# Landmark attention and two MLPs on one Trainium2 core: stores on another queue, less elementwise work on GpSimd, one chain for the inverse

## Chip, cores and metric

The kernel runs on one core of a Trainium2 chip. The metric is device time in microseconds (us). TensorE (PE) multiplies matrices, VectorE (DVE) and ScalarE (ACT) work elementwise, GpSimd (POOL) does some elementwise steps and issues transfers, SyncE (SP) only issues transfers.

## What is computed

Three stages follow one another; the output of one is the input of the next.

```python
# attention, B, H, S, D = 4, 8, 576, 64; 32 landmarks, each the mean of 18 rows
A  = softmax(scale * q    @ k_lm.T)      # 576 x 32 per head
Bm = softmax(scale * q_lm @ k_lm.T)      # 32 x 32
C  = softmax(scale * q_lm @ k.T)         # 32 x 576
Z  = Bm.T / (norm1(Bm) * norminf(Bm) + 1e-6)
for _ in range(6):
    Z = 2 * Z - Z @ Bm @ Z               # approximate inverse of Bm
x = A @ Z @ C @ v                        # heads side by side: 2304 x 512
# first MLP, 512 -> 1536 -> 512
x = (sigmoid(x @ w_gate) * (x @ w_val)) @ w_out
# second MLP, 512 -> 2048 -> 512
h = x @ w_in
out = (max(h, 0) + alpha * min(h, 0)) @ w_out2
```

The weights arrive as 8-byte floats; the rest is 4-byte.

## The kernel before

**Attention.** It runs per batch b, in two groups j of four heads. `transposed` brings k and q into a transposed layout and forms the landmark means. `landmark_scores` and `landmark_exp` give Bm; `att_values` gives C @ v (tile Cv); `att_queries` gives A, split into two float32r parts. `newton(b, j)` computes the inverse of one group: after a preamble of small VectorE steps, six steps, each with four 32-row matmuls on the diagonal (L396), a ScalarE copy (L426) and a VectorE add (L427, the last one L432). Z and Cv are multiplied to M (L442). A and M are never multiplied with the weights of the first MLP apart: `fold` forms We = M @ w (matmul L578), so that layer 1 is A @ We.

For batch 0 the six parts (inverse, queries, values, each for two groups) are interleaved by `together`, one yield of each in turn. The attention of later batches is spread over the blocks of the first MLP, a pace setting how many yields go into one block; the inverse of these has a higher priority in the scheduler (`urgent`). Each engine takes its instructions in a fixed order that the scheduler worked out at build time from program order, priorities and its own estimates.

**Weights.** Each 8-byte weight tile is loaded by SP (`raw`) and narrowed to 4 bytes by `narrow`: one or two ScalarE steps (L128, L132), and on VectorE L137 and L140, with L134 in place of L132 for some. `split` makes two float32r parts: a ScalarE cast (L113) and a subtraction (L114) that goes to VectorE or, with `lo="pool"`, to GpSimd. The gate and value weights are also stored in DRAM (`wgvd`, L556) and reloaded for later batches by GpSimd's queue (L564). The folded weights of batch 3 are stored (`we3d`) and taken back by `take_stored`. `narrow_w2` prepares the second MLP's weights during the first: load, narrow into tile n, store to `w2d` (L670).

**First MLP.** There are 24 blocks per batch (12 column chunks f for each of two halves of 288 rows). A block is `layer1` (12 matmuls, L616), the sigmoid (L627), a product (L628) and a split, then `layer2` (12 matmuls, L635) two blocks later. Finished tiles xs are stored to `x2d` (L726). **Second MLP**: `load_x2` reads x2d and splits it (the subtraction on GpSimd), `layer3` (L812) and `layer4` (L830) follow.

Before the change every store is issued on SP's queue, in which the loads also stand, and an issue that waits holds what is behind it. The code that the change touches:

Of the kernel before, what the change touches and what calls it, by code (L numbers as in the profile page):

```python
# [21 lines left out]
def tile_landmark_attention_glu_prelu(  # L22
# [240 lines left out]
    def value_scores(b, j, ps_tile):  # L263
# [4 lines left out]
        for half in range(2):  # L268
# [10 lines left out]
    def value_exp(b, j):  # L279
# [6 lines left out]
        for half in range(2):  # L286
            nc.scalar.activation(
                e[:, half * HB : (half + 1) * HB], pc[half][:, :HB], AF.Exp,
                bias=mx[:, 2:3], scale=SCALE, accum_out=den[:, half : half + 1],
            )  # L290
# [45 lines left out]
    def query_scores(b, j, ps_tile):  # L336
# [21 lines left out]
    def query_rest(b, j):
# [28 lines left out]
    def newton(b, j, ps_tile):  # L387

        bm = att[b, j, "B"]
        bt = apool.tile([P, LM], F32, tag="bt", name="bt", bufs=2)  # L390
        nc.vector.transpose(out=bt, in_=bm)

        def diag(ps, lhsT, rhs, n):
            for h in range(4):
                s = slice(32 * h, 32 * h + 32)
                nc.tensor.matmul(ps[s, :n], lhsT=lhsT[s], rhs=rhs[s], start=True, stop=True)  # L396

        pb = ps_tile("psbb")
        diag(pb, bm, bm, LM)
        sums = apool.tile([P, 2], F32, tag="sums", name="sums", bufs=2)  # L400
        nc.vector.tensor_reduce(out=sums[:, 0:1], in_=bm, axis=AX.X, op=ALU.add)
        nc.vector.tensor_reduce(out=sums[:, 1:2], in_=bt, axis=AX.X, op=ALU.add)
        st = apool.tile([P, 2, LM], F32, tag="st", name="st", bufs=2)
        sp = apool.tile([P, 2, LM], F32, tag="sp", name="sp", bufs=2)
        nc.vector.tensor_copy(sp, sums[:, :, None].to_broadcast([P, 2, LM]))
        nc.vector.transpose(
            out=st.rearrange("p a l -> p (a l)"), in_=sp.rearrange("p a l -> p (a l)")
        )
        nm = apool.tile([P, 2], F32, tag="nm", name="nm", bufs=2)
        nc.vector.tensor_reduce(out=nm, in_=st, axis=AX.X, op=ALU.max)  # L410
        nr = apool.tile([P, 1], F32, tag="nr", name="nr", bufs=2)
        nc.vector.tensor_scalar(
            out=nr, in0=nm[:, 0:1], scalar1=nm[:, 1:2], scalar2=1e-6, op0=ALU.mult, op1=ALU.add
        )
# [1 line left out]
        rz = apool.tile([P, 2, LM], F32, tag="rz", name="rz", bufs=4)
        nc.vector.tensor_scalar(out=rz[:, 1], in0=bt, scalar1=nr, scalar2=None, op0=ALU.mult)
        nc.vector.tensor_scalar(out=rz[:, 0], in0=pb[:, :LM], scalar1=nr, scalar2=None, op0=ALU.mult)
        nc.vector.tensor_tensor(out=rz[:, 0], in0=eye, in1=rz[:, 0], op=ALU.subtract)
# [497 lines left out]
```

## Time and profile before

| | |
|---|---|
| median of 3 runs | 903.42 us (900.98 to 907.16) |
| the profiled execution | 905.6 us, span 903.8 us, mean granted TensorE clock 0.969 |
| PE busy | 856.2 us (95%) |
| DVE busy | 519.8 us (58%) |
| ACT busy | 339.3 us (38%) |
| POOL busy | 98.1 us (11%) |
| DMA | 106.92 MB, mean 118 GB/s |

The span runs from the first to the last instruction. The rows further down name a line of the kernel, an engine, an operation and its tiles as output<-input; "[... <-X]" at the end of a row is the time for which the engine had been idle just before, and the instruction that ended the wait.

### The profile page before, as it was taken

How to read it: one execution, taken by the hardware profiler on the slowest of the kernel's cores; microseconds unless marked ns; L12 is line 12 of the kernel's file. 1: busy time of each engine (PE TensorE's matmuls, PEld its weight loads, DVE VectorE, ACT ScalarE, POOL GpSimd, SP SyncE). 2: the span in 40 equal slices, each digit the busy share in tenths (PEclk: the TensorE clock that was granted, in tenths of full speed). 3: DMA queues.
4: the chain of work that ended last, by engine and by line, in shares of the span. 5: the costliest groups of instructions: out<-in, count | busy, mean ns of one | idle time of the engine just before them, and what ended most of it. 6: DMA issues, size and time to landing. Idle time of an engine off the chain costs nothing.

```text
span 903.8 us, 15276 instructions
## 1 busy us (share of the span) xinstructions
PE 856.2 (95%) x5969; PEld 705.6 (78%) x5969; DVE 519.8 (58%) x1113; ACT 339.3 (38%) x729; POOL 98.1 (11%) x98
## 2 busy tenths in 40 slices
PE   5789888989999999999999999999999999999997
PEld 3347666757778877998899888888888888888896
DVE  5789998668767443576745653443344433444443
ACT  4755856357745433555434421121112111111111
POOL 3301313111111010124100020110010001000000
PEclk8589999979999999999999999999999999999999
DMA  9767777787523252687824420030002000100100
GB/s 257 214 212 233 218 251 203 261 250 229 175 56 103 72 166 95 208 292 231 273 78 119 153 71 1 2 91 1 1 24 58 1 1 12 48 0 1 28 20 24
DMA packets 85161, 106.92 MB, mean 118 GB/s; under 512 B 35664, under 2 KB 57184, under 8 KB 85088
## 3 DMA queue, kind: packets, MB, share of 16 engines
q1 hardware_dynamic: 81632, 93.36, 34.5%
q0 software_dynamic: 3456, 12.58, 4.4%
q8 instruction: 47, 0.77, 0.4%
q14 instruction: 26, 0.21, 0.1%
HBM read 78.65 MB, written 27.26 MB: 117 GB/s over the span
## 4 chain that ended last, share of the span: by engine, by line
PE 76%; DMA 11%; DVE 8%; issue 2%; ACT 1%; POOL 1%; SPq 0%; DVEq 0%; POOLq 0%; ACTq 0%
PE h L812 22%; PE o L830 22%; PE gv L616 12%; PE acc L635 11%; DMA raw<-in_moe_w_out_dram 4%; PE psf L578 4%; DMA raw<-in_moe_w_val_dram 2%; DMA w2d<-n 2%; DVE raw L137 1%; DMA raw<-in_moe_w_in_dram 1%; PE psz L396 1%; DMA tv<-in_v_dram 1%; DVE n L140 1%; PE psa L218 1%; PE psq L191 1%
## 5 line engine op out<-in xcount | busy, mean ns | idle before, releaser
L616 PE MATMUL gv<-A,we 128*128 128x288 f32 x1152 | 194.6, 308 | 7.0 <-ACT g L627 5.4
L616 PEld LDWEIGHTS gv<-A,we 128*128 128x128 f32 x1152 | 164.4, 193 | 41.2 <-issue 27.9
L635 PE MATMUL acc<-gs,wconv 128*128 128x288 f32 x1152 | 184.2, 302 | 6.6 <-DVE gs L114 4.8
L812 PE MATMUL h<-x,w 128*128 128x512 f32 (+1 forms) x840 | 183.7, 368 | 0.0
L635 PEld LDWEIGHTS acc<-gs,wconv 128*128 128x128 f32 x1152 | 162.9, 191 | 19.5 <-issue 10.6
L830 PE MATMUL o<-w,g2s 128*128 128x512 f32 x702 | 170.0, 389 | 0.0
L812 PEld LDWEIGHTS h<-x,w 128*128 128x128 f32 x840 | 148.0, 188 | 27.2
L830 PEld LDWEIGHTS o<-w,g2s 128*128 128x128 f32 x702 | 131.0, 188 | 26.6
L113 ACT CAST g2s<-g 128x512 fp32r<-128x512 f32 (+1 forms) x80 | 46.3, 578 | 276.3 <-DVE g L822 276.3
L818 DVE TENSOR_SCALAR g<-h,alphaT 128x512 f32<-128x512 f32 (+1 forms) x80 | 55.8, 697 | 154.0 <-PE h L812 153.9
L114 DVE TENSOR_TENSOR g2s<-g,g2s 128x512 fp32r<-128x512 f32 (+1 forms) x80 | 55.9, 699 | 55.9 <-ACT g2s L113 55.3
L628 DVE TENSOR_TENSOR g<-g,gv 128x288 f32<-128x288 f32 x96 | 43.0, 448 | 34.4 <-PE gv L616 30.6
L128 ACT ACTIVATE raw<-raw 128x512 f32<-128x512 f32 x68 | 46.6, 686 | 41.2 <-DMA raw<-in_moe_w_in_dram 19.2
L114 DVE TENSOR_TENSOR gs<-g,gs 128x288 fp32r<-128x288 f32 x96 | 48.7, 508 | 21.6 <-ACT gs L113 20.8
L114 POOL TENSOR_TENSOR x<-xr,x 128x512 fp32r<-128x512 f32 (+1 forms) x20 | 24.1, 1218 | 315.3 <-ACT x L113 315.3
L627 ACT ACTIVATE g<-gv 128x288 f32<-128x288 f32 x96 | 39.4, 410 | 47.3 <-PE gv L616 44.9
L137 DVE SCALAR_TENSOR_TENSOR raw<-raw 128x512 uint32<-128x512 uint32 x68 | 51.1, 758 | 9.8 <-ACT raw L132 8.8
L113 ACT CAST gs<-g 128x288 fp32r<-128x288 f32 x96 | 41.4, 432 | 40.5 <-DVE g L628 40.4
L822 DVE SCALAR_TENSOR_TENSOR g<-h,g 128x512 f32<-128x512 f32 (+1 forms) x80 | 51.0, 638 | 2.7
L578 PE MATMUL psf<-wgv,m 64*32 64x512 f32 x384 | 46.2, 629 | 2.2 <-DVE ta L343 1.4
L114 DVE TENSOR_TENSOR we<-psf,we 128x512 fp32r<-128x512 f32 x36 | 23.9, 687 | 19.3 <-ACT we L113 19.2
L113 ACT CAST we<-psf 128x512 fp32r<-128x512 f32 x36 | 20.1, 587 | 32.1 <-PE psf L578 32.1
(134 smaller groups left out, 761.1 us busy)
## 6 DMA issues: line engine op xcount, KB each, us to landing
raw<-in_moe_w_out_dram SPq DMA_DIRECT2D x28, 512.0 KB, 5.8
wgv<-wgvd POOLq DMA_DIRECT2D x24, 512.0 KB, 5.8
raw<-in_moe_w_in_dram SPq DMA_DIRECT2D x16, 512.0 KB, 5.1
w2d<-n SPq DMA_DIRECT2D x32, 256.0 KB, 2.8
st<-w2d SPq DMA_DIRECT2D x32, 256.0 KB, 2.7
raw<-in_moe_w_gate_dram SPq DMA_DIRECT2D x24, 256.0 KB, 4.1
raw<-in_moe_w_val_dram SPq DMA_DIRECT2D x24, 256.0 KB, 4.6
wgvd<-wgv SPq DMA_DIRECT2D x12, 512.0 KB, 6.1
```

Source lines behind the costliest of these rows:

```text
L113: nc.scalar.copy(dst[:, 0, :], src)
L114: (nc.gpsimd if lo == "pool" else nc.vector).tensor_tensor(out=dst[:, 1, :], in0=src, in1=f32(dst[:, 0, :]), op=ALU.subtract)
L128: nc.scalar.activation(w[:, :, 1], w[:, :, 1], AF.Copy, scale=2.0 ** -112)
L137: nc.vector.scalar_tensor_tensor(out=lo, in0=hi, scalar=0x80000000, in1=lo, op0=ALU.bitwise_and, op1=ALU.bitwise_or)
L578: nc.tensor.matmul(pss[j][LM * h : LM * h + LM], lhsT=att[b, j, "M"][d, u], rhs=wgv[c, j][d, u], start=True, stop=True,)
L616: nc.tensor.matmul(ps[:, :HB], lhsT=We[b, c, j][:, a, 256 * i + P * s : 256 * i + P * s + P], rhs=att[b, j, "A"][half][:, e, :], start=(n ...
L628: nc.vector.tensor_tensor(out=g, in0=g, in1=pss[1][:, :HB], op=ALU.mult)
L635: nc.tensor.matmul(acc[m][:, :HB], lhsT=wout_sb[f][:, a, P * m : P * m + P], rhs=gs[:, e, :], start=(f == f0 and n == 0), stop=(f == f1 - ...
L812: nc.tensor.matmul(ps[:, :n], lhsT=w[:, a, kk], rhs=xs[:, e, kk, :n], start=(i == 0), stop=(i == 11))
L818: nc.vector.tensor_scalar(out=g[:, :n], in0=ps[:, :n], scalar1=0.0, scalar2=alphaT[:, f : f + 1], op0=ALU.min, op1=ALU.mult,)
L822: nc.vector.scalar_tensor_tensor(out=g[:, :n], in0=ps[:, :n], scalar=0.0, in1=g[:, :n], op0=ALU.max, op1=ALU.add)
L830: nc.tensor.matmul(acc, lhsT=gs[:, a, P * t : P * t + P], rhs=w2_out[f][:, e, :], start=(f == 0 and i == 0), stop=(f == NF2 - 1 and i == 2),)
```

## The change

It has these parts.

1. The stores of wgvd, we3d, w2d and x2d are issued by GpSimd's queue in place of SP's.
2. The first MLP's splits and the attention's subtraction and product (L349, L365) go from GpSimd to VectorE; only the splits of `load_x2` stay on GpSimd.
3. In batch 0 the `tok` copies go from VectorE to ScalarE, and the landmark sums are one VectorE reduction over all 576 columns; before, GpSimd added two halves first.
4. The landmarks stay sums: the division by 18 (L208) moves into the scales of the exponentials.
5. `newton` takes both groups, eight heads, in each step, with instructions of twice the width; in batch 0 it has the higher priority, and values come before queries.
6. Tile n (`n2`) always has two buffers; it had one until the attention's pool is released.

```diff
@@ -178,9 +180,7 @@
 
         if b == 0:
             tv = apool.tile([TP, R, 2, D], F32, tag="qkv", name="tok", bufs=4)
-            nc.vector.tensor_copy(
-                tv, pre.pop((nm[0], pr)).rearrange("p h (r d) -> p r h d", r=R)
-            )
+            nc.scalar.copy(tv, pre.pop((nm[0], pr)).rearrange("p h (r d) -> p r h d", r=R))
         else:
             tv = load_pair_tok(src, b, pr, "t" + nm)
         x = small_or_slot(b, [P, S + LM], "qT", nm, 4)
@@ -194,19 +194,11 @@
                     ident[:TP, :TP],
                 )
             nc.scalar.copy(x[:, half * HB : (half + 1) * HB], ps[:, :HB])
-        sm = apool.tile([P, LM], F32, tag="lsum", name="lsum", bufs=2)
-        xr, nr = x[:, :S], R
-        if b == 0:
-            xr, nr = apool.tile([P, HB], F32, tag="xh", name="xh", bufs=2), RH
-            nc.gpsimd.tensor_tensor(out=xr, in0=x[:, :HB], in1=x[:, HB:S], op=ALU.add)
         nc.vector.tensor_reduce(
-            out=sm,
-            in_=xr.rearrange("p (r l c) -> p l r c", r=nr, c=TP // LM),
+            out=x[:, S:],
+            in_=x[:, :S].rearrange("p (r l c) -> p l r c", r=R, c=TP // LM),
             axis=AX.XY,
             op=ALU.add,
-        )
-        nc.vector.tensor_scalar(
-            out=x[:, S:], in0=sm, scalar1=1.0 / G, scalar2=None, op0=ALU.mult
         )
         return x
...
@@ -346,14 +339,14 @@
         t3 = ta.rearrange("p (n l) -> p n l", l=LM)
         am = apool.tile([P, G], F32, tag="am", name="am", bufs=2)
         nc.vector.tensor_reduce(out=am, in_=t3, axis=AX.X, op=ALU.max)
-        nc.gpsimd.tensor_tensor(
+        nc.vector.tensor_tensor(
             out=t3, in0=t3, in1=am[:, :, None].to_broadcast([P, G, LM]), op=ALU.subtract
         )
         att[b, j, "qs"] = ta
 
     def query_exp(b, j):
         ta = att[b, j, "qs"]
-        nc.scalar.activation(ta, ta, AF.Exp, scale=SCALE)
+        nc.scalar.activation(ta, ta, AF.Exp, scale=SCALE1)
 
     def query_rest(b, j):
         ta = att.pop((b, j, "qs"))
@@ -362,14 +355,14 @@
         nc.vector.tensor_reduce(out=asum, in_=t3, axis=AX.X, op=ALU.add)
         nc.vector.tensor_scalar(out=asum, in0=asum, scalar1=1e-9, scalar2=None, op0=ALU.add)
         nc.vector.reciprocal(out=asum, in_=asum)
-        nc.gpsimd.tensor_tensor(
+        nc.vector.tensor_tensor(
             out=t3, in0=t3, in1=asum[:, :, None].to_broadcast([P, G, LM]), op=ALU.mult
         )
         at = apool.tile([P, S], F32, tag="T", name="at", bufs=3)
         nc.vector.transpose(out=at, in_=ta)
         if b < B - 1:
             a2 = bpool.tile([P, 2, S], F32R, tag="A", name="A", bufs=4)
-            split(a2, at, lo="pool" if b == 0 else "dve")
+            split(a2, at)
             att[b, j, "A"] = [a2[:, :, h * HB : (h + 1) * HB] for h in range(2)]
         else:
             att[b, j, "A"] = []
...
@@ -384,68 +377,97 @@
-    def newton(b, j, ps_tile):
+    def newton(b, ps_tile):
+        bm = att.pop((b, "B"))
...
+        def diag(ps, lhsT, rhs):
+            for j in range(2):
+                for h in range(4):
+                    s = slice(32 * h, 32 * h + 32)
+                    to = ps[s, j]
+                    nc.tensor.matmul(to, lhsT=lhsT[s, j], rhs=rhs(s, j), start=True, stop=True)
...
         for i in range(6):
-            ps = ps_tile("psz")
-            zn = apool.tile([P, 2, LM], F32, tag="rz", name="rz", bufs=4)
             if i < 5:
-                diag(ps, rz[:, 0], rz.rearrange("p a l -> p (a l)"), 2 * LM)
-                nc.scalar.copy(zn[:, 0], ps[:, :LM])
-                nc.vector.tensor_tensor(
-                    out=zn[:, 1], in0=rz[:, 1], in1=ps[:, LM : 2 * LM], op=ALU.add
-                )
+                zn = small("rz", 2, 2, LM)
+                ps = psum("psz", 2, 2, LM)
+                diag(ps, rz[:, :, 0], lambda s, j: rz[s, j])
+                nc.scalar.copy(zn[:, :, 0], ps[:, :, 0])
+                zj, pz = zn[:, :, 1], ps[:, :, 1]
             else:
-                diag(ps, rz[:, 0], rz[:, 1], LM)
-                nc.vector.tensor_tensor(out=zn[:, 1], in0=rz[:, 1], in1=ps[:, :LM], op=ALU.add)
+                zj = small("zs", 2, LM)
+                pz = psum("psz", 2, LM)
+                diag(pz, rz[:, :, 0], lambda s, j: rz[s, j, 1])
+            nc.vector.tensor_tensor(out=zj, in0=rz[:, :, 1], in1=pz, op=ALU.add)
             rz = zn
             yield
-        zt = apool.tile([P, LM], F32, tag="zt", name="zt", bufs=2)
-        nc.vector.transpose(out=zt, in_=rz[:, 1])
-
-        pm = [ps_tile(f"psm{u}") for u in range(2)]
-        cv = att[b, j, "Cv"]
-        for u, hh, h in HEADS[j]:
-            s = slice(h * LM, h * LM + LM)
-            nc.tensor.matmul(
-                pm[u][D * hh : D * hh + D, :LM], lhsT=cv[s], rhs=zt[s], start=True, stop=True
-            )
-        m = apool.tile([P, 2, LM], F32, tag="m", name="m", bufs=4)
-        for u in range(2):
-            nc.vector.tensor_copy(m[:, u], pm[u][:, :LM])
-        att[b, j, "M"] = m
+        zt = turned("zt", zj, 2)
...
@@ -510,7 +531,8 @@
         yield from together(*(att_landmarks(0, j, ps_tile) for j in range(2)))
         raw_ahead(RAW0)
         yield from together(
-            *(part(0, j, ps_tile) for part in (newton, att_queries, att_values) for j in range(2))
+            urgent(newton(0, ps_tile)),
+            *(part(0, j, ps_tile) for part in (att_values, att_queries) for j in range(2)),
         )
 
 
@@ -545,7 +567,7 @@
         raw = raws.pop((kind, c, pr))
         if kind == "o":
             t = wout_sb[c] = ws_tile("wconv")
-            split(t, narrow(raw), lo="dve" if c in LO_DVE else "pool")
+            split(t, narrow(raw))
             return
         j, u = divmod(pr, 2)
         if u == 0:
@@ -553,7 +575,7 @@
         t = wgv[c, j]
         narrow(raw, t[:, u], act=True)
         if u == 1:
-            nc.sync.dma_start(out=wgvd[c, j], in_=t)
+            nc.gpsimd.dma_start(out=wgvd[c, j], in_=t)
         if pr == NK - 1:
             take(0, c, fold(0, c, bank))
 
@@ -594,14 +616,14 @@
         for j in range(2):
             st = apool.tile([P, NW], F32, tag="T", name="st", bufs=3)
             (nc.vector.tensor_copy if j else nc.scalar.copy)(st, pss[j])
-            nc.sync.dma_start(out=we3d[c, j], in_=st)
+            nc.gpsimd.dma_start(out=we3d[c, j], in_=st)
 
     def take_stored(c):
         for j in range(2):
             st = qpool.tile([P, NW], F32, tag="xr", name="st3", bufs=2)
             nc.sync.dma_start(out=st, in_=we3d[c, j])
             We[B - 1, c, j] = ws_tile("we3")
-            split(We[B - 1, c, j], st, lo="pool")
+            split(We[B - 1, c, j], st)
 
     wout_sb = {}
 
@@ -665,9 +687,9 @@
             )
         else:
             nc.sync.dma_start(out=raw, in_=w_out2[P * f : P * f + P, :])
-        t = pool.tile([P, NW], F32, tag="n2", name="n2", bufs=1 if rpool is None else 2)
+        t = pool.tile([P, NW], F32, tag="n2", name="n2", bufs=2)
         narrow(raw, t, act=which == 0)
-        nc.sync.dma_start(out=w2d[i], in_=t)
+        nc.gpsimd.dma_start(out=w2d[i], in_=t)
 
     def convert_w2(i):
         t = rpool.tile([P, NW], F32, tag="st2", name="st2", bufs=2)
@@ -723,7 +745,7 @@
             else:
                 (nc.vector.tensor_copy if m % 2 else nc.scalar.copy)(to, got)
             if f1 == NF1:
-                nc.sync.dma_start(out=x2d[2 * b + half][:, m], in_=to)
+                nc.gpsimd.dma_start(out=x2d[2 * b + half][:, m], in_=to)
 
     for b in range(B):
         if b == 0:
```

## Rows read from the trace of the kernel before

**Rows 1.** The page: busy us, share of the span and instructions of each engine.
```profile
PE 856.2 (95%) x5969; PEld 705.6 (78%) x5969; DVE 519.8 (58%) x1113; ACT 339.3 (38%) x729; POOL 98.1 (11%) x98
```

**Rows 2.** Busy time by long stretch: stretch, width, engines, granted clock, DMA share, GB/s.
```profile
24.10:52.45 28.35, 20.29 (x293) 9.55 (x292) 20.36 (x81) 15.83 (x41) 7.93 (x6) 0.56 0.73 208
52.45:158.00 105.55, 93.57 (x764) 68.46 (x765) 95.25 (x216) 70.96 (x150) 21.72 (x18) 0.97 0.75 223
158.00:226.00 68.00, 63.19 (x586) 49.45 (x586) 49.28 (x126) 35.39 (x80) 7.98 (x13) 0.92 0.79 247
...
300.00:426.00 126.00, 123.70 (x1068) 106.88 (x1066) 67.52 (x136) 57.21 (x130) 19.83 (x18) 1.00 0.55 177
```

**Rows 3.** The same view around the holes: PE, PEld, DVE, ACT, POOL, clock, DMA.
```profile
92.00:96.00 4.00, 1.99 (x15) 1.75 (x15) 4.00 (x8) 3.22 (x10) 1.32 (x2) 1.00 0.76 243
108.00:116.00 8.00, 5.79 (x35) 5.55 (x34) 8.00 (x16) 5.05 (x11) 2.56 (x2) 0.79 0.61 165
132.00:136.00 4.00, 1.98 (x13) 1.52 (x12) 4.00 (x9) 1.96 (x4) 1.07 (x2) 1.00 0.74 233
152.00:160.00 8.00, 6.79 (x75) 5.53 (x73) 6.75 (x31) 2.61 (x10) 3.94 (x5) 0.79 0.97 273
180.00:192.00 12.00, 8.61 (x55) 7.49 (x54) 8.07 (x17) 5.53 (x13) 0.00 (x0) 0.72 0.77 243
196.00:204.00 8.00, 6.58 (x43) 3.25 (x36) 6.38 (x11) 4.75 (x8) 2.20 (x3) 0.79 0.77 259
```

**Rows 4.** Timeline (start, duration, instruction) around 180 us, VectorE and TensorE.
```profile
178.58 0.69 DVE L140 SCALAR_TENSOR_TENSOR n<-raw 128x512 uint32<-128x512 uint32 x1 [3.79 <-DMA w2d<-n]
...
183.38 1.34 PE L191 MATMUL psq<-ident,tkT 96*128 96x96 f32 x6 [3.35 <-DVE we L114]
```

**Rows 5.** Timeline of VectorE and GpSimd: VectorE steps beside GpSimd's.
```profile
57.40 1.44 DVE L140 SCALAR_TENSOR_TENSOR wgv<-raw 128x512 uint32<-128x512 uint32 x1
...
92.00 1.32 POOL L114 TENSOR_TENSOR wconv<-raw,wconv 128x512 fp32r<-128x512 f32 x1
92.26 1.61 DVE L137 SCALAR_TENSOR_TENSOR raw<-raw 128x512 uint32<-128x512 uint32 x1
...
154.67 0.49 DVE L427 TENSOR_TENSOR rz<-rz,psz 128x32 f32<-128x32 f32 x2
```

**Rows 6.** Groups by form, VectorE, whole span: count, busy us, mean ns.
```profile
L114 DVE TENSOR_TENSOR A<-at,A 128x576 fp32r<-128x576 f32 x4 | 3.0, 751 | 0.0
...
L114 DVE TENSOR_TENSOR wconv<-raw,wconv 128x512 fp32r<-128x512 f32 x2 | 1.4, 675 | 0.0
```

**Rows 7.** Timeline of TensorE in the first attention: inverse and first layer 1.
```profile
28.78 0.31 PE L396 MATMUL psz<-rz 32*32 32x64 f32 x8 [1.68 <-DVE mx L274]
...
46.65 0.43 PE L442 MATMUL psm<-zt,cv 32*64 32x32 f32 x8 [1.74 <-DVE zt L436]
...
52.45 2.71 PE L616 MATMUL gv<-A,we 128*128 128x288 f32 x12
```

**Rows 8.** VectorE, first attention: inverse groups (24.10 to 52.45), and one timeline row.
```profile
L427 DVE TENSOR_TENSOR rz<-rz,psz 128x32 f32<-128x32 f32 x10 | 1.6, 171 | 2.2 <-ACT rz L426 2.2
...
L432 DVE TENSOR_TENSOR rz<-rz,psz 128x32 f32<-128x32 f32 x2 | 0.3, 174 | 0.0
...
21.07 0.17 DVE L208 TENSOR_SCALAR qT<-lsum 128x32 f32<-128x32 f32 x1
```

**Rows 9.** Groups by form, ScalarE, whole span.
```profile
L356 ACT ACTIVATE ta<-ta 128x576 f32<-128x576 f32 x8 | 5.5, 682 | 2.0 <-POOL ta L349 2.0
```

**Rows 10.** Timeline of TensorE near the end of the first MLP.
```profile
425.50 1.88 PE L635 MATMUL acc<-gs,wconv 128*128 128x288 f32 x12 [1.36 <-DVE gs L114]
```

**Rows 11.** Waits of SyncE's queue, 25 to 52 us: total, times, longest.
```profile
SPq L556 <- DVE rz L427: 11.1, 1, 11.1
```

**Rows 12.** GpSimd: waits from 150 to 345 us, and its transfer issues by form.
```profile
POOL wgv L564 <- PE gv L616: 56.4, 8, 14.1
...
L564 POOL DMA_DIRECT2D wgv<-wgvd x24 | 13.2, 550 | 99.3 <-PE gv L616 56.4 <-PE psf L578 42.2 <-DVE xs L722 0.8
```

More of the change, by code (lines that the diff above doesn't have):

```diff
@@ L274, in value_scores @@
         nc.vector.tensor_scalar(
-            out=mx[:, 2:3], in0=mx[:, 2:3], scalar1=-SCALE, scalar2=None, op0=ALU.mult
+            out=mx[:, 2:3], in0=mx[:, 2:3], scalar1=-SCALE1, scalar2=None, op0=ALU.mult
         )
@@ L288, in value_exp @@
                 e[:, half * HB : (half + 1) * HB], pc[half][:, :HB], AF.Exp,
[L289 removed]
+                bias=mx[:, 2:3], scale=SCALE1, accum_out=den[:, half : half + 1],
             )
@@ L385, in att_queries @@
         yield
-    def newton(b, j, ps_tile):
[L389 to L407, printed above, removed]
-        )
[L409 to L413, printed above, removed]
-        )
@@ new lines, in newton, with small, turned, psum @@
+    def newton(b, ps_tile):
+        bm = att.pop((b, "B"))
+        def small(name, *shape):
+            return apool.tile([P, *shape], F32, tag=name, name=name, bufs=2 if name == "rz" else 1)
+        def turned(name, src, n):
+            t = small(name, *src.shape[1:])
+            flat = " ".join("abc"[: len(src.shape) - 1])
+            nc.vector.transpose(
+                out=t.rearrange(f"p {flat} -> p ({flat})"),
+                in_=src.rearrange(f"p {flat} -> p ({flat})"),
+            )
+            return t
+        def diag(ps, lhsT, rhs):
[4 more added lines that the diff above has]
+                    nc.tensor.matmul(to, lhsT=lhsT[s, j], rhs=rhs(s, j), start=True, stop=True)
+        def psum(name, *shape):
+            n = 1
+            for k in shape:
+                n *= k
+            t = ps_tile(name)[:, :n]
+            if len(shape) == 3:
+                return t.rearrange("p (j a l) -> p j a l", j=shape[0], a=shape[1])
+            return t.rearrange("p (j l) -> p j l", j=shape[0])
+        bt = turned("bt", bm, 2)
+        pb = psum("psbb", 2, LM)
+        diag(pb, bm, lambda s, j: bm[s, j])
+        sums = small("sums", 2, 2)
+        nc.vector.tensor_reduce(out=sums[:, 0], in_=bm, axis=AX.X, op=ALU.add)
+        nc.vector.tensor_reduce(out=sums[:, 1], in_=bt, axis=AX.X, op=ALU.add)
+        sp = small("sp", 4, LM)
+        nc.vector.tensor_copy(
+            sp, sums.rearrange("p a j -> p (a j)")[:, :, None].to_broadcast([P, 4, LM])
+        )
+        st = turned("st", sp, 4)
+        nm = small("nm", 2, 2)
+        nc.vector.tensor_reduce(
+            out=nm.rearrange("p a j -> p (a j)"), in_=st, axis=AX.X, op=ALU.max
+        )
+        nr = small("nr", 2)
+        nc.vector.tensor_tensor(out=nr, in0=nm[:, 0], in1=nm[:, 1], op=ALU.mult)
+        nc.vector.tensor_scalar(out=nr, in0=nr, scalar1=1e-6, scalar2=None, op0=ALU.add)
@@ L415, in newton @@
         nc.vector.reciprocal(out=nr, in_=nr)
[L416 to L419, printed above, removed]
+        nrb = nr[:, :, None].to_broadcast([P, 2, LM])
+        rz = small("rz", 2, 2, LM)
+        nc.vector.tensor_tensor(out=rz[:, :, 0], in0=pb, in1=nrb, op=ALU.mult)
@@ L446, in newton @@
-        for u in range(2):
-            nc.vector.tensor_copy(m[:, u], pm[u][:, :LM])
-        att[b, j, "M"] = m
+        zt = turned("zt", zj, 2)
+        for j in range(2):
+            pm = [ps_tile(f"psm{u}") for u in range(2)]
+            cv = att.pop((b, j, "Cv"))
+            for u, hh, h in HEADS[j]:
+                s = slice(h * LM, h * LM + LM)
+                nc.tensor.matmul(
+                    pm[u][D * hh : D * hh + D, :LM], lhsT=cv[s], rhs=zt[s, j],
+                    start=True, stop=True,
+                )
+            m = apool.tile([P, 2, LM], F32, tag="m", name="m", bufs=4)
+            for u in range(2):
+                nc.vector.tensor_copy(m[:, u], pm[u][:, :LM])
+            att[b, j, "M"] = m
@@ L473, in attention @@
             yield from att_group(b, j, ps_tile)
-        yield from together(*(urgent(newton(b, j, ps_tile)) for j in range(2)))
+        yield from urgent(newton(b, ps_tile))
     def att_group(b, j, ps_tile):
@@ L500, in later_attentions @@
         yield from att_group(B - 1, 1, ps_tile)
-        yield from together(*(urgent(newton(B - 1, j, ps_tile)) for j in range(2)))
+        yield from urgent(newton(B - 1, ps_tile))
     def first_attention(ps_tile):
```

22 lines of the change are left out of this document (14 added, 8 removed).

## The prediction, made before the change was run

> **What bounds the kernel now.** I read the page from the outside in. The engine line shows TensorE busy for 95% of the span [rows 1]: at most 48 us are idle, and the question is where they lie. The table of long stretches answers it [rows 2]. From 300 to 426 us TensorE is busy for 123.70 of 126 us at a granted clock of 1.00 (2.4 GHz; 0.50 is 1.2), so nothing that another engine does there can move the end by much. The loss lies earlier. From 24.10 to 52.45, the second half of the first attention, TensorE runs at a granted clock of 0.56 and waits for results; the first layer-1 matmul starts only at 52.45 [rows 7]. From 52.45 to 158 VectorE is busy 95.25 of 105.55 us (90%) while TensorE has 12 us idle. From 158 to 226 VectorE has room (49.28 of 68), yet TensorE loses 4.8 us idle and runs at 0.92. After 226 TensorE hardly pauses, so what is won before it moves the end one for one.
>
> Next I cut the two middle stretches into pieces to find the holes [rows 3]. Counting width less busy time times clock, the loss is 2.0 us in 92 to 96, 3.4 in 108 to 116, 2.0 in 132 to 136, 2.6 in 152 to 160, 5.8 in 180 to 192, 2.8 in 196 to 204. The first four hold VectorE at full or nearly full load and a GpSimd tensor_tensor each; the fifth holds no GpSimd work at all.
>
> The timelines tell why. At 92.00 GpSimd splits a weight for 1.32 us, and the VectorE step L137 issued at 92.26 takes 1.61 us, ending with GpSimd's instruction plus its usual 0.6 to 0.7 [rows 5]. So a VectorE step with two SBUF operands is held while GpSimd runs one. From 52.45 to 158 ten VectorE steps are stretched so, from 1.44 for 0.69 at 57.40 to 0.49 for 0.3 at 154.67 [rows 5]; their excess over the usual times sums to 8.3 us. The fifth hole is another matter: VectorE stands idle 3.79 us for the landing of an earlier store of the narrowed weight n, since that tile has one buffer, and TensorE then lacks We for 3.35 us [rows 4].
>
> **The first attention, 0 to 52.45 us.** Eight tok copies leave VectorE for ScalarE, where no such copy is shown. The nearest row, 576 columns at 0.682 us [rows 9], bounds it below; scaled to 768 columns it is 0.91, and I take that, since the row grows with its columns: 7.3 us more on ScalarE while the tiles arrive. Tiles come over some 8 us there, so part of it is late: 0 to 3 us. In return GpSimd's eight pair sums and VectorE's L208 go, the last of which ran only at 21.07, behind a weight conversion [rows 8]. I set these against each other and take nothing (2 lost to 2 won).
>
> The inverse has two interleaved chains of four heads, from the first psz matmul at 28.78 to psm at 46.65 [rows 7]: 17.9 us for six steps, 3.0 a step, because every small step sits between query and value work. Afterwards one chain of eight heads has priority. Its matmul count is the same; VectorE's 14 groups of inverse steps sum to 6.6 us for two chains, from 1.6 for L427 to 0.3 for L432 [rows 8], and one chain of double width should cost about 1.2 times one of the two (estimate: 64 columns against 32 hardly lengthen a step of 0.2), 4.1 with its extra step, so 2.5 less. Against that VectorE takes over two subtractions, two products and two splits of 576 columns, for which the split of the same shape takes 0.751 [rows 6]: 4.5 us more. The held steps in this stretch give back about 1.4. VectorE's 20.36 us become 21.0. The stretch is 28.35; it can't fall below 21.0 unless conversions slip behind it, and at worst it stays. With VectorE idle 4 us instead of 8.0 it is 25: **3.5 us won** (0 to 7). The value path goes first now; the next thing to be late is the query path, whose A is needed by the first gv.
>
> **52.45 to 158.** To VectorE come ten weight splits at 0.675 [rows 6], 6.8 us, and four query steps at 0.75, 3.0. Away go the 8.3 us of holding, eight L208 at 0.17 [rows 8], 1.4, and half of one inverse, 1.8. The balance is -1.7: 93.6 us. If VectorE keeps its 90%, the stretch shrinks by 1.8; if all four holes close it shrinks by 10.0, and VectorE would be 98% full, which I don't believe. I take half, **5 us** (0 to 10), because the removed round trips sat right at the holes. What is late next is VectorE's own queue: g, gs and we steps behind conversions.
>
> **158 to 226.** With two n buffers the wait of 3.79 goes, and We comes in time. That hole cost 5.8; I take **5 us**. The 2.8 of 196 to 204 belong to a transpose queued on VectorE, and I leave them. With a GpSimd product gone, VectorE gains nothing to speak of here.
>
> **226 to 500.** Twelve splits of the stored We go to VectorE, 8.1 us where it has room; the hold before the 1.36 us gap at 425.50 [rows 10] goes: **1 us**. The next gaps, at 430, follow splits of the second layer's input, which stay on GpSimd.
>
> **The stores.** 88 move from SyncE's queue to GpSimd's: 12 of gate/value weights, 12 of folded ones, 32 narrowed ones, 32 of x2. SyncE is freed of waits such as the 11.1 us before one store [rows 11], during which loads stood behind it. I count no gain for that, because the holes above name no late load. On GpSimd an issue takes 0.550 us [rows 12], so 48 us more of issuing on an engine that was busy 98.1 us in all [rows 1] and loses most of its elementwise steps: nothing on the path, as long as no store waits behind a reload (below).
>
> A rule speaks against this move. The trace shows 24 GpSimd issues at a mean of 0.550 amid all of VectorE's work [rows 12], and I add nothing. The Trainium skill, SBUF — State Buffer (section "SBUF: two separate sides"), warns that a DMA issued from GpSimd starves for descriptors while VectorE runs a copy in its two-port mode. By it, each store would land some tenths of a us later; the sum stays as it is, since a second buffer lies behind each of the stores that anything waits for.
>
> **The sum.** 3.5 + 5 + 5 + 1 = 14.5 us. The profiled execution took 905.6 (span 903.8 and 1.8 around it), which gives 891.1; the median of the runs is 903.42, 2.2 below it, so 888.9. **Forecast: 889** (882 to 895 by itself), chance 0.51.
>
> **Rivals.**
> *VectorE eats it* (0.26). At 90% load the ten splits and four query steps land in front of g and gs, new holes replace the old ones, and the longer ScalarE part delays the landmarks. Then 0 to 1 us in the first attention, nothing to 158, 5 in the n buffer: 903.4 - 5.5 = 898 (895 to 903). For it: VectorE is full in three of the four holes. Against: what it gives up is as much as what it takes.
>
> *All holes close* (0.14). 7 in the attention, 10.0, 5.8, 2.8 and 1.4 give 27.0: 876 (870 to 882). For it: TensorE is saturated behind. Against: VectorE at 98%.
>
> *Stores stuck behind reloads: slower* (0.09). GpSimd's queue runs in order, and its reloads of wgv already wait for slots: 8 of these waits for TensorE sum to 56.4 us, 7.1 each [rows 12]. An n store that stands behind such a wait leaves its buffer full; the second buffer covers perhaps half, so VectorE is held for 3.5 us, about the wait that cost 5.8 before, say 5 each. Five such stores cost 25, less the 9.5 of the other terms: 919 (905 to 919). It decides from three stores on. Against: the order is planned, and a store is placed ahead of a reload whose slot comes later.
>
> That the change doesn't do what it says: the eight-head chain could stay as slow as before, if TensorE's queue puts value and query matmuls between its steps anyway. Then the first term is 0, time 892, inside the forecast's own range.
>
> **How the numbers follow.** About 1% (9 us) is what a measurement of this kernel can tell from no change. Faster (under 894.4): 0.46 of the forecast and 0.14 of the large gain, 0.60. Within: 0.26, 0.05 of the forecast's upper end and 0.03 of the slow rival's lower end, 0.34. Slower: 0.06. The range 877 to 902 leaves out some 0.07 of the large gain and the slow rival's 0.09.
>
> **What would show it.** Right: first gv matmul near 49; no VectorE step L137 or L140 over 1 us before 158; no wait of VectorE for the landing of n; six inverse steps in some 12 us; 226 us of before reached about 13 earlier and the rest parallel. Wrong: TensorE waiting for g or gs of VectorE just as long between 60 and 158; GpSimd stores issued many us after their data; the landmarks' exponentials later than 22.5.

## The result and the profile after

The changed kernel takes **914.76 us** (median of 4 runs, 911.58 to 916.17) against 903.35 for the kernel before in the same job: ratio 1.0121, 95% interval 1.009 to 1.0153. It is slower by 11.4 us, and the forecast of 889 was wrong in its sign. The profiled execution took 916.17 us, its span 914.4.

The page's engine line after the change, to hold against [rows 1]:

```profile
PE 861.6 (94%) x5969; PEld 713.0 (78%) x5969; DVE 511.9 (56%) x1045; ACT 336.9 (37%) x711; POOL 85.7 (9%) x138
```

VectorE took over GpSimd's steps and is yet busy for 7.9 us less. The same long stretches as in [rows 2], and the one behind them:

```profile
24.10:52.45 28.35, 19.02 (x287) 9.79 (x286) 24.48 (x69) 20.31 (x43) 1.23 (x2) 0.68 0.98 274
52.45:158.00 105.55, 96.72 (x706) 72.25 (x707) 87.07 (x193) 64.52 (x136) 7.83 (x14) 0.89 0.68 214
158.00:226.00 68.00, 62.07 (x624) 47.16 (x623) 51.64 (x120) 36.12 (x82) 15.31 (x28) 0.97 0.79 241
226.00:300.00 74.00, 68.93 (x736) 56.39 (x731) 46.09 (x139) 37.57 (x89) 5.43 (x10) 0.98 0.42 117
300.00:426.00 126.00, 124.32 (x1093) 106.23 (x1093) 68.25 (x145) 55.62 (x123) 20.66 (x38) 1.00 0.51 167
```

VectorE's load from 52.45 to 158 fell from 95.25 to 87.07 us, but the clock fell too, 0.97 to 0.89. From 226 to 300, where I expected no loss, TensorE is idle for 5.1 us; before, it was idle for 1.7:

```profile
226.00:300.00 74.00, 72.31 (x797) 58.76 (x795) 51.14 (x172) 45.55 (x104) 9.55 (x10) 1.00 0.40 116
```

Timeline of TensorE in the first attention, beside [rows 7]:

```profile
29.82 0.43 PE L403 MATMUL psz<-rz 32*32 32x64 f32 x16
...
42.55 0.47 PE L463 MATMUL psm<-zt,cv 32*64 32x32 f32 x16 [0.71 <-DVE zt L392]
...
49.62 1.58 PE L638 MATMUL gv<-A,we 128*128 128x288 f32 x10 [1.95 <-DVE A L116]
```

The inverse takes 12.7 us instead of 17.9, and layer 1 sets in at 49.62 (two early matmuls stand at 46.82) instead of 52.45. VectorE's groups by form from 52.45 to 158, the first line from the kernel before (they answer to the holding of [rows 5]), then GpSimd's issues of the whole span (to [rows 12]):

```profile
L137 DVE SCALAR_TENSOR_TENSOR raw<-raw 128x512 uint32<-128x512 uint32 x29 | 22.5, 789 | 0.5 <-ACT raw L132 0.4
```

```profile
L139 DVE SCALAR_TENSOR_TENSOR raw<-raw 128x512 uint32<-128x512 uint32 x28 | 18.9, 688 | 0.0
L142 DVE SCALAR_TENSOR_TENSOR wgv<-raw 128x512 uint32<-128x512 uint32 x20 | 13.5, 687 | 0.0
```

```profile
L692 POOL DMA_DIRECT2D w2d<-n x32 | 17.6, 551 | 118.7 <-DVE n L142 101.0 <-DVE sp L421 9.7 <-DVE rd L285 6.1
...
L586 POOL DMA_DIRECT2D wgv<-wgvd x24 | 13.1, 549 | 64.4 <-ACT g L649 40.7 <-PE gv L638 17.0 <-PE psf L600 6.2
```

The mean of L139 (L137 before) is 688 ns instead of 789: no step of it is held any more. An issue costs 551 ns, as before (550). A new hole shows where a part of the time goes, in the timelines of three engines around 230 us:

```profile
229.69 0.43 DVE L136 TENSOR_SCALAR raw<-raw 128x512 uint32<-128x512 uint32 x1 [4.54 <-DMA raw<-in_moe_w_out_dram]
...
236.86 0.67 ACT L130 ACTIVATE raw<-raw 128x512 f32<-128x512 f32 x1 [4.72 <-DMA raw<-in_moe_w_in_dram]
...
230.77 0.69 PE L210 MATMUL psa<-qT,kT 64*32 64x288 f32 x8 [1.38 <-DVE we L116]
...
233.69 0.69 PE L210 MATMUL psc<-kT,qT 64*32 64x288 f32 x8 [0.94 <-DVE ta L336]
...
241.70 1.29 PE L299 MATMUL pse<-ident,e 128*96 128x128 f32 x6 [2.50 <-ACT e L280]
```

VectorE no longer waits for the landing of a store of n [rows 4]; it and ScalarE wait for the loads of the second MLP's weights, and steps that TensorE needs at once (we, ta, e) stand behind the waiting ones in their lists.

### The profile page after: what moved, and what is told of

Its sections match the earlier page's. It is cut to its first block, busy times and chain, and to the rows that moved or that the text cites. A ratio compares the mean times of both kernels' runs of the same rounds, so it can differ in the third digit from the quotient of the medians.

```text
span 914.4 us, 15144 instructions
## 1 busy us (share of the span) xinstructions
PE 861.6 (94%) x5969; PEld 713.0 (78%) x5969; DVE 511.9 (56%) x1045; ACT 336.9 (37%) x711; POOL 85.7 (9%) x138
## 4 chain that ended last, share of the span: by engine, by line
PE 67%; DMA 13%; issue 7%; DVE 6%; ACT 5%; SPq 1%; POOL 0%; ACTq 0%; DVEq 0%; POOLq 0%
PE o L852 21%; PE h L834 21%; PE gv L638 9%; PE acc L657 8%; DMA raw<-in_moe_w_in_dram 5%; DMA st<-w2d 3%; DMA raw<-in_moe_w_out_dram 3%; PE psf L600 2%; PE psq L191 1%; ACT raw L130 1%; DMA tk<-in_k_dram 1%; PE psz L403 1%; DVE raw L139 1%; ACT raw L134 1%; DVE we L116 1%
## 5 line engine op out<-in xcount | busy, mean ns | idle before, releaser
L638 PE MATMUL gv<-A,we 128*128 128x288 f32 x1152 | 200.0, 313 | 7.2 <-ACT g L649 3.8
L638 PEld LDWEIGHTS gv<-A,we 128*128 128x128 f32 x1152 | 167.4, 196 | 40.2 <-issue 21.0
L657 PEld LDWEIGHTS acc<-gs,wconv 128*128 128x128 f32 x1152 | 165.3, 194 | 20.8 <-issue 8.5
L650 DVE TENSOR_TENSOR g<-g,gv 128x288 f32<-128x288 f32 x96 | 43.3, 451 | 41.1 <-PE gv L638 38.4
L116 DVE TENSOR_TENSOR gs<-g,gs 128x288 fp32r<-128x288 f32 x96 | 45.1, 470 | 23.7 <-ACT gs L115 23.4
L139 DVE SCALAR_TENSOR_TENSOR raw<-raw 128x512 uint32<-128x512 uint32 x68 | 46.3, 689 | 9.8 <-ACT raw L134 8.0
L116 DVE TENSOR_TENSOR we<-psf,we 128x512 fp32r<-128x512 f32 x36 | 23.7, 685 | 17.6 <-ACT we L115 17.4
```

Of the source, the lines that this page charges most:

```text
L116: (nc.gpsimd if lo == "pool" else nc.vector).tensor_tensor(out=dst[:, 1, :], in0=src, in1=f32(dst[:, 0, :]), op=ALU.subtract)
L139: nc.vector.scalar_tensor_tensor(out=lo, in0=hi, scalar=0x80000000, in1=lo, op0=ALU.bitwise_and, op1=ALU.bitwise_or)
L638: nc.tensor.matmul(ps[:, :HB], lhsT=We[b, c, j][:, a, 256 * i + P * s : 256 * i + P * s + P], rhs=att[b, j, "A"][half][:, e, :], start=(n ...
L650: nc.vector.tensor_tensor(out=g, in0=g, in1=pss[1][:, :HB], op=ALU.mult)
L657: nc.tensor.matmul(acc[m][:, :HB], lhsT=wout_sb[f][:, a, P * m : P * m + P], rhs=gs[:, e, :], start=(f == f0 and n == 0), stop=(f == f1 - ...
```

## The experiments

**First: which part costs?** Theory Q blames the stores' queue, V VectorE's added load, A the new attention.

only_queue: the kernel before, its 88 stores on GpSimd's queue.
```diff
-nc.sync.dma_start(out=w2d[i], in_=t)      # likewise wgvd, we3d, x2d
+nc.gpsimd.dma_start(out=w2d[i], in_=t)
```


> The kernel before with nothing changed but the issuing queue of the 88 stores. Theory Q (the stores' queue: with SyncE freed, loads are issued in bunches beside GpSimd's stores and reloads, land later than ScalarE and VectorE meet their first use, and these wait in order): slower than before, 908 to 916. Theory V (VectorE's added elementwise steps cost the time) and theory A (the attention's new form costs it later on): within 1% of before, 899 to 907.

Measured: 922.49 us, ratio 1.0206 (1.0173 to 1.024), slower even than Q said.

only_elem: the kernel before, with `split(...)` without `lo="pool"` and L349, L365 on VectorE.


> The kernel before with nothing changed but the elementwise steps of the first MLP and the attention's subtraction and product going from GpSimd to VectorE (the first attention's pair sums stay on GpSimd). Theory V: slower, 908 to 918. Theory Q and theory A: faster or equal, 896 to 904, since the held VectorE steps go (8.3 us of them before 158 us).

Measured: 905.62, 1.0031 (1.0009 to 1.0052), between the two ranges and near the lower.

only_attn: the kernel before, with parts 3 to 5 of the change alone.


> The kernel before with the attention's new form alone (tok copies on ScalarE, one reduction, no division, eight heads per step of the inverse, values before queries); stores, splits, subtraction, product and the n buffer as before. Theory A: slower than before, 908 or more, with first layer 1 still 3 to 4 us earlier. Theory Q and theory V: 897 to 902, the 4 us that the first layer 1 came earlier in the changed kernel and no later loss.

Measured: 903.7, 1.0005 (0.9983 to 1.0027), also between the two.

undo_queue: the changed kernel, its stores back on SyncE.
```diff
-nc.gpsimd.dma_start(out=w2d[i], in_=t)    # likewise wgvd, we3d, x2d
+nc.sync.dma_start(out=w2d[i], in_=t)
```


> The changed kernel with all 88 stores back on SyncE's queue. Theory Q: the loss goes and the forecast gain appears, 888 to 900. Theory V and theory A: the loss stays, 908 to 918.

Measured: **896.99**, 0.9941 (0.9917 to 0.9965). So the stores cost 17.8 us (914.76 - 896.99; about 16 by the two ratios), and the rest of the change gains 5.3 (by the ratio, of 902.6 in that job). Q holds in its direction, V and A fall.

**Second: which stores?** In each of three kernels one class moves from undo_queue's SyncE to GpSimd's queue (uq_n: n; uq_w: wgvd and we3d; uq_x: x2d); in n_sync all but n. Here N, S, W name the stores of n, SyncE's freed loads and the weights' stores.

> The changed kernel with only the 32 stores of n on GpSimd's queue, the other 56 on SyncE's. Theory N (the stores of n do it: they stand among GpSimd's reloads and free SyncE exactly where the next 8-byte load should be issued): 908 to 916. Theory S (each class of stores contributes, because SyncE's loads are issued earlier and in bunches whatever store is gone): 900 to 906. Theory W (the gate, value and folded weights' stores do it): 894 to 900, like all stores on SyncE's queue.

> The changed kernel with only the 24 stores of gate, value and folded weights on GpSimd's queue. Theory W: 908 to 916. Theory S: 900 to 906. Theory N: 894 to 900.

> The changed kernel with only the 32 stores of x2 on GpSimd's queue. Theory N and theory W: 894 to 900. Theory S: 899 to 905. If the splits of the second layer's input on GpSimd hold these stores back (one wait of 2.79 us at 439 us in the changed kernel), 900 to 903 as well.

> The changed kernel with the 32 stores of n back on SyncE's queue, the other 56 on GpSimd's. Theory N: 894 to 900. Theory W: 908 to 916. Theory S: 903 to 909.

Measured: uq_n **913.7** (1.0115, 1.0074 to 1.0155), uq_w 900.15 (0.996, 0.994 to 0.998), uq_x 898.03 (0.9946, 0.9928 to 0.9963), n_sync 904.0 (1.0006, 0.9981 to 1.003). The n stores alone cost 16.7 (of 17.8 for all); the others 3.2 and 1.0 alone but 7.0 together. So N names the main part, n_sync falls in the range of S, and the parts don't add up.

**Third: is GpSimd's queue held?** In uq_n the wgv reloads stand behind n stores that wait for L142, and come out in pairs while a raw load runs. That became theory H; P is a dearer path for the bytes.

pool_hold: undo_queue, and
```diff
+hold = pool.tile([P, 1], F32, tag="hold", name="hold", bufs=2)
+nc.gpsimd.tensor_copy(hold, t[:, :1])     # behind each store of n
```


> The changed kernel with all its stores back on SyncE's queue (897.0 measured), and added to it one GpSimd copy of the first column of each narrowed weight n: GpSimd's queue waits for the step L142 that makes n, as a store of n there did, but moves no store. The copy is extra work whose output nothing reads. Theory H (the order: GpSimd's queue is held by the wait for n, the reloads of wgv behind it come out bunched and meet the next raw load): most of the 17 us of the run with only the n stores on GpSimd (913.7) come back, 906 to 914, reloads in pairs and raw loads of over 8 us as there. Theory P (the path: the stores themselves are dearer from GpSimd's queue, landing in 4.9 us instead of 2.8): no more than 899.

Measured: 897.35, 0.9955 (0.9912 to 0.9998). H falls: GpSimd waits for n and pairs the reloads, and nothing is lost.

reload_sync: the changed kernel, wgv reloads on SyncE.


> The changed kernel, all 88 stores on GpSimd's queue, with the reloads of wgv issued on SyncE's instead, so that no reload stands behind a store of n. Theory H: the loss of 18 us against the stores on SyncE (897.0) is mostly gone, 897 to 905, unless SyncE's queue is now held by reloads that wait for a slot, which would show as raw loads issued late behind them. Theory P: as the changed kernel, 911 to 917, since every store still takes GpSimd's path.

Measured: 904.45, 1.0011 (0.9993 to 1.0029). Read alone it would have confirmed H.

uq_n1 (undo_queue, `n2` with one buffer again) and attn_n2 (undo_queue without the elementwise move) size two terms of the forecast.


> The changed kernel with its stores back on SyncE (897.0), and the narrowed weight n with one buffer again, as in the kernel before. My forecast had 5 us for the second buffer: 902. If the wait for the landing of n was covered by other slack: 897 to 898, with VectorE's wait of some 3.8 us for n back in the trace.

> The kernel before with the new form of the attention and the second buffer of n: splits, subtraction and product stay on GpSimd, stores on SyncE. It lacks of the 897.0 kernel only the move of the elementwise steps. My forecast had 5 us for that move from 52 to 158 us and 1 after 226: 903. If the move is worth nothing by itself (alone it gave 905.6 against 902.6): 895 to 898.

Measured: uq_n1 896.12 (0.9919, 0.9893 to 0.9945), attn_n2 902.74 (1.0003, 0.998 to 1.0025).

**Fourth: the written order.** Beside undo_queue's, the instruction lists of the built kernels show more. uq_n differs not only on two queues: 87 of VectorE's 1045 instructions and 58 of TensorE's matmuls stand elsewhere in their lists. pool_hold's lists are those of undo_queue on every engine but GpSimd. The table gives, for the seventh to twelfth and the last narrowing of a second-MLP weight, the number of g products (L650) that stand before its last step (L142) in VectorE's list:

| | 7 | 8 | 9 | 10 | 11 | 12 | 32 |
|---|---|---|---|---|---|---|---|
| undo_queue, sp_pace | 24 | 25 | 26 | 27 | 30 | 32 | 80 |
| uq_n | 23 | 24 | 25 | 27 | 27 | 30 | 77 |
| changed kernel | 23 | 24 | 25 | 26 | 27 | 29 | 77 |

sp_pace: uq_n, and where the whole store stood SyncE stores one row; the lists of TensorE, VectorE and ScalarE are then undo_queue's:
```diff
 nc.gpsimd.dma_start(out=w2d[i], in_=t)
+nc.sync.dma_start(out=pacer[i], in_=t[:1, :])
```


> The changed kernel with the stores of gate, value, folded weights and x2 on SyncE, the stores of n on GpSimd (913.7 measured), and for each of these one added store of a single row of n on SyncE at the place where the whole store stood. With that the written order of TensorE, VectorE, ScalarE and SyncE is, step by step, that of the kernel with all stores on SyncE (897.0); GpSimd's queue alone has 32 issues more. The 32 single-row stores are extra work. Theory W (the loss comes from the written order, which the scheduler changed when SyncE lost these stores): 896 to 901. Theory G (the loss comes from GpSimd's queue: wgv reloads held behind stores of n, stores and reloads sharing the DMA engines with the raw loads): 909 to 915. In between, both.

Measured: **896.32**, 0.9917 (0.9888 to 0.9946). Every byte of n goes through GpSimd's queue, reloads stand behind the stores, and the 17 us are gone.

pool_pace: the mirror, whole store on SyncE, one row on GpSimd; the lists of TensorE, VectorE and ScalarE are again undo_queue's.


> The mirror of the run before: the whole stores of n stand on SyncE, and GpSimd issues a single row of each. Every engine's written order is the same as there, so GpSimd's queue waits for n at the same places with the wgv reloads behind; only the bytes of n go the other way. Theory W: as there, 896 to 901. Theory G with the hold as its cause: as there, 909 to 915. Theory G with the path of the bytes as its cause: 897 to 900 here and 909 to 915 there.

Measured: 900.29, 0.9969 (0.9945 to 0.9993): no 909 to 915 here either, if some 3 us above undo_queue, with intervals that overlap, and 4.0 above sp_pace in the same job, with intervals that just touch. So even between kernels with these same lists some 3 or 4 us are unexplained, and differences of that size say little.

uqn_reload: uq_n, wgv reloads on SyncE.


> The kernel with only the n stores on GpSimd's queue (913.7), its wgv reloads moved to SyncE, so that nothing stands behind the n stores but the last stage's splits. Theory G by the hold: 897 to 902. Theory W: open in size, since the order is written anew; if the loss stays, 908 to 915, the reloads were not its cause.

Measured: 898.31, 0.9945 (0.992 to 0.997). The figure fits H, but the lists changed again: the seventh to twelfth narrowing now stand behind 26 to 35 products, later than in undo_queue.

uq_tok: undo_queue, tok copies of batch 0 on VectorE.


> The kernel with all stores on SyncE (897.0), and of the leaner attention one step undone: the eight tok copies of batch 0 are back on VectorE, which stands idle up to 14.85 us while ScalarE copies from 7.40 to 14.89 and only then starts on the kT copies. My forecast took 2 us for the copies on ScalarE. If that was right: 895. If the tiles' arrival sets the start: 896.5 to 897.5.

Measured: 902.09, 0.9992 (0.9968 to 1.0016): 5.1 us slower, against both expectations.

all_pace: the changed kernel, and for each of its 88 stores a small one of the same tile on SyncE.


> The changed kernel with all its 88 stores on GpSimd's queue (914.8 measured), and for each an added store of part of one row of the same tile on SyncE, at the place where the whole store stood in the kernel with all stores on SyncE (897.0). The written order is then near that kernel's (the 32 narrowings of n stand within one block of it, where the changed kernel's stand up to four blocks earlier). The 88 small stores are extra work. Theory W (the written order): 895 to 903, though every byte and every wait of the change's stores is on GpSimd's queue. Theory G (that queue itself, for the other three classes of stores or for their sum): 908 to 916.

Measured: 906.12, 1.0034 (1.0011 to 1.0056), between the two: 8.6 us come back, 9.1 do not.

uq_nact: undo_queue, n stores on ScalarE's queue.


> The kernel with all stores on SyncE (897.0), its n stores moved to ScalarE's queue instead of GpSimd's. GpSimd holds no store here and its reloads go as they come free. SyncE loses the n stores as it did when they went to GpSimd (913.7), and the scheduler again writes the narrowings of n earlier, by one to four blocks. Theory W: 905 to 915. Theory G: 897 to 901, the 32 issues on ScalarE counted.

Measured: 902.47, 1.0003 (0.9977 to 1.003), again between: 5.5 us are lost although GpSimd holds no store. The 32 issues, some 0.34 us each, now stand in ScalarE's list, so this is not a run of the rewritten lists alone.

**The hole, with and without the order.** The twelfth narrowing in uq_n, in the timelines of SyncE, VectorE and TensorE, and then the busy time around it:

```profile
214.38 2.41 SPq L154 DMA_DIRECT2D vt<-in_v_dram  x2
217.43 1.33 SPq L163 DMA_DIRECT2D tkT<-in_k_dram  x2
219.81 1.24 SPq L163 DMA_DIRECT2D tqT<-in_q_dram  x2
221.14 2.72 SPq L689 DMA_DIRECT2D raw<-in_moe_w_out_dram  x1
...
232.55 0.43 DVE L136 TENSOR_SCALAR raw<-raw 128x512 uint32<-128x512 uint32 x1 [6.70 <-DMA raw<-in_moe_w_out_dram]
232.89 0.47 DVE L336 STREAM_TRANSPOSE ta<-psa 128x288 f32<-128x288 f32 x1
233.29 0.15 DVE L224 TENSOR_REDUCE bmx<-psb 128x1 f32<-128x32 f32 x1
...
233.42 1.18 PE L210 MATMUL psc<-kT,qT 64*32 64x288 f32 x8 [6.07 <-DVE ta L336]
```

```profile
228.00:232.00 4.00, 0.00 (x0) 0.00 (x0) 0.00 (x0) 0.00 (x0) 0.00 (x0) 1.00 0.80 294
232.00:240.00 8.00, 6.58 (x36) 4.46 (x37) 5.39 (x16) 5.20 (x11) 0.00 (x0) 0.57 0.01 5
```

The raw load is issued behind the attention's loads at 221.14 and lands 11.4 us later. L136 stands first in VectorE's list, so the transpose L336 and the step of the scores' bound behind it wait with it; all four computing engines stand still from 228 to 232, and then TensorE runs 8 us at 0.57, near the lower of its two levels (0.50 is 1.2 GHz): 1.18 us for what takes 0.69 below. The same narrowing in sp_pace:

```profile
217.94 0.48 SPq L692 DMA_DIRECT2D pacer<-n  x1
...
219.02 0.67 SPq L689 DMA_DIRECT2D raw<-in_moe_w_out_dram  x1
...
223.22 0.48 DVE L336 STREAM_TRANSPOSE ta<-psa 128x288 f32<-128x288 f32 x1 [0.51 <-PE psb L210]
...
230.42 0.42 DVE L136 TENSOR_SCALAR raw<-raw 128x512 uint32<-128x512 uint32 x1
...
223.87 0.69 PE L210 MATMUL psc<-kT,qT 64*32 64x288 f32 x8
```

```profile
222.00:228.00 6.00, 6.00 (x60) 4.31 (x60) 4.65 (x15) 3.86 (x9) 0.00 (x0) 1.00 0.73 275
228.00:230.00 2.00, 2.00 (x17) 1.86 (x16) 2.00 (x7) 1.98 (x6) 0.55 (x1) 1.00 0.00 1
```

The load is issued at 219.02, and the step that needs it runs 11.4 us later here too, without a wait: in this list the transpose, the query's maximum and more stand ahead of it. The load is asked for later there. It was also quicker: no DMA engine is busy from 228 to 230, so it had landed by 228, within 9 us of its issue. How much the order brings here and how much the quicker load is not separated. The sixth narrowing is the other such hole; in uq_n and then in sp_pace:

```profile
186.10 0.43 DVE L136 TENSOR_SCALAR raw<-raw 128x512 uint32<-128x512 uint32 x1 [5.31 <-DMA raw<-in_moe_w_out_dram]
185.13 0.43 DVE L136 TENSOR_SCALAR raw<-raw 128x512 uint32<-128x512 uint32 x1 [0.41 <-DMA raw<-in_moe_w_out_dram]
```

In uq_n this step stands one g product earlier, and VectorE reaches it at 180.79 instead of 184.72. Its load, issued at 175.20 instead of 179.66, lands 1.0 us later all the same, and TensorE waits 5.70 us. Waits for raw loads from 160 to 260 us, in uq_n and then in sp_pace (engine, tile, releaser: total, times, longest):

```profile
ACT raw L130 <- DMA raw<-in_moe_w_out_dram: 14.4, 4, 7.2
DVE raw L136 <- DMA raw<-in_moe_w_out_dram: 12.0, 2, 6.7
ACT raw L130 <- DMA raw<-in_moe_w_in_dram: 5.0, 5, 1.7
```

```profile
ACT raw L130 <- DMA raw<-in_moe_w_in_dram: 8.0, 5, 3.2
ACT raw L130 <- DMA raw<-in_moe_w_out_dram: 1.4, 2, 1.1
DVE raw L136 <- DMA raw<-in_moe_w_out_dram: 0.4, 1, 0.4
```

That the hold itself was there in sp_pace, its GpSimd timeline shows (one of the reload pairs, released with a store of n):

```profile
187.82 0.55 POOL L692 DMA_DIRECT2D w2d<-n  x1 [7.67 <-DVE n L142]
188.41 1.07 POOL L586 DMA_DIRECT2D wgv<-wgvd  x2
```

Progress agrees. Layer-1 matmuls (L638) by stretch, in uq_n and then in sp_pace:

```profile
52.45:158.00 105.55, 40.48 (x213) 32.41 (x214) 0.96 0.71 224
158.00:226.00 68.00, 24.22 (x125) 18.59 (x123) 0.95 0.84 248
226.00:300.00 74.00, 28.73 (x144) 21.23 (x145) 0.95 0.33 95
```

```profile
52.45:158.00 105.55, 42.08 (x214) 33.68 (x214) 0.93 0.71 224
158.00:226.00 68.00, 25.45 (x135) 19.80 (x134) 0.97 0.86 261
226.00:300.00 74.00, 31.79 (x162) 23.22 (x163) 1.00 0.32 91
```

Equal to 158; by 300 uq_n is 28 matmuls behind, 13 us at sp_pace's rate of 162 in 74 us. (A few per cent of the records may be missing, and the engine's other work is not counted; the figure is rough.) TensorE's busy time and clock from 160 to 260, in uq_n and then in sp_pace, say the same:

```profile
160.00:260.00 100.00, 85.44 (x866) 0.93 0.71 209
160.00:260.00 100.00, 94.34 (x971) 0.98 0.70 210
```

Width less busy time times clock, the prediction's measure of a hole, is 20.5 us there in uq_n and 7.5 in sp_pace: 13.0 of the 17.4 us between the two kernels.

## Why the prediction was wrong

**The step that failed is the stores, counted at 0** ("nothing on the path, as long as no store waits behind a reload"). They cost 17.8 us. I costed the move on the queues: 88 issues of 550 ns, the order of two queues. The chip bears that costing out where it can be seen by itself: with the lists and SyncE's waits of undo_queue, the n stores on GpSimd's queue cost nothing (896.32 to 896.99). What I left out is that the engines' lists are worked out anew when a queue changes. SyncE without its n stores gave another plan, in which narrowings stand up to three products earlier, and two of them met loads that had not landed.

Four of the five signs that I had named for being right came true (first gv near 49, no long L139 or L142, no wait for the landing of n, six inverse steps in 12 us) in a kernel 25.8 us slower than forecast: none of them looks at a load. Nor do the stores make up the whole miss. With them on SyncE the kernel takes 896.99, still 8 us above 889 and outside the 882 to 895 of the forecast by itself: two other terms show no gain at the end, the 3.5 of the attention and the 5 of the buffer (below).

How far this is shown: for the n stores, the runs exclude GpSimd's queue, by the hold (pool_hold) and by the bytes (sp_pace). The one-row stores bring back two things at once, the lists and SyncE's own waits for n in front of the next raw loads; these two the runs do not part. An earlier place in the list is the mechanism seen in uq_n's holes, not a general law: in only_queue the eighth narrowing moved from 24 to 28 products, later, and the time still rose 18.6 us (by its ratio). And of the changed kernel's loss, 9.1 us remain in all_pace. The count of L638 does not say where; from 52.45 to 158, in all_pace and then in uq_w:

```profile
52.45:158.00 105.55, 38.86 (x200) 29.93 (x200) 0.96 0.70 223
52.45:158.00 105.55, 41.59 (x192) 32.03 (x192) 0.90 0.68 214
```

undo_queue has 218 in that stretch, the changed kernel 194. all_pace is behind, but uq_w is further behind and ends only 3.2 us above undo_queue. In all_pace 83 of VectorE's instructions and 123 of TensorE's matmuls still stand elsewhere than in undo_queue; whether those lists or GpSimd's queue cost the 9 us is open.

**First attention, 3.5 us.** Right in its mechanism, near in its size: 2.8 in the changed kernel, six steps in 12 us, exponentials at 21.90, before the 22.5 that would have refuted it; VectorE is busy for 24.48 us of that stretch, though, not 21.0. But the form gained nothing at the end, neither alone (only_attn, 903.7: the first gv there stands at 51.34 and the lead goes again behind it) nor with the second buffer (attn_n2, 902.74). The set-off "2 lost to 2 won" for the tok copies is open: ScalarE's copy takes 0.83 (I took 0.91), and uq_tok, with them back on VectorE, is 5.1 us slower, though the landmark sums begin sooner there, at 13.52 us instead of 14.85; its list is another, so the 5.1 are not the copies' price. Its TensorE waits for A longer than undo_queue's 2.95 us at 50.11:

```profile
54.60 1.81 PE L638 MATMUL gv<-A,we 128*128 128x288 f32 x6 [4.27 <-DVE A L116]
```

**52.45 to 158, and 1 us after 226.** Right in size: undo_queue is 5.7 us below attn_n2, whose source lacks only this move; I had 5 + 1. But the lists differ here too, so the 5.7 are the move with its new lists, and where they were won is not shown. By itself on the kernel before it cost 2.8 us (only_elem, by its ratio), so the price holds only beside the other parts. The Trainium skill, SBUF — State Buffer (section "SBUF: two separate sides"), has VectorE and GpSimd share a port; the trace agrees: with GpSimd's steps gone the mean of L139 (L137 before) in that stretch is 688 ns against 789, and none is over 1 us.

**The second n buffer, 5 us.** Wrong: uq_n1, with one buffer, takes 896.12, no more than 896.99. VectorE's wait is back there, and the end does not see it:

```profile
DVE n L142 <- DMA w2d<-n: 5.6, 2, 4.4
```

I took the whole hole of 5.8 [rows 3, 4] for the buffer's; what it gives does not reach the end.

**The rivals.** The time came out near the slow rival's (919, 905 to 919), to which I gave 0.09, but not by its mechanism: VectorE never waited for a store of n to land, and 29 of the 32 issues of n follow the end of their L142 by 0.3 us, the other three by 1.1 to 1.2. In uq_n, the slow one, all 32 follow by 0.3. "All holes close" (876) falls with undo_queue. "VectorE eats it" (898) has undo_queue's 896.99 in its range, but by chance: it gave the elementwise move nothing and the buffer 5, and uq_n1 and attn_n2 show it the other way round. The median n store lands in 4.9 us against 2.8 before, and in 4.7 in sp_pace, which loses nothing. The rule of the Trainium skill (same page and section), that a DMA issued from GpSimd starves while VectorE copies, could account for part of that, which no run here separates; by it the sum stays, and sp_pace agrees.

The version to keep is the change with its stores on SyncE (896.99) or with n's pacing row (896.32): some 0.6 to 0.8% below the kernel before.

## What to carry to other kernels

Where a scheduler writes every engine's list, moving a transfer to another queue is not an edit of two queues: compare the lists before and after, and price the steps that changed place, above all those that wait for a load and stand ahead of what TensorE needs. To test a queue by itself, keep the lists the same: a one-row store in the old place did that here for the stores of n, though not for all 88. Runs whose lists differ (reload_sync, uqn_reload, uq_tok) moved by 5 to 15 us, and their edits' own share can't be read from them: two of them seemed to confirm a theory that fell.

## What the hardware showed unexpectedly

A wait of 6.07 us on TensorE was paid for again: after it the granted clock was 0.57 for 8 us, 6.58 of them busy, which is 2.8 us more than at full clock. And GpSimd's queue could be held by a store for 7.67 us, its reloads released in pairs, without any loss.
